# Four small moves in a fused attention and feed-forward kernel: first weight loads, idle products, the keys' cast, and where the first tile is stored

## The chip, the cores and the metric

One core of a Trainium2 chip runs the kernel. The metric is the device time of one execution in microseconds. The profile is of one execution; the times are medians of several. With one core there is no other core's clock to compare with, so a run counts as "fast" when it is within 1.5% of the fastest of its kernel; all comparisons below use fast runs.

## The reference, cut to what matters

```python
# q, k, v: (8, 8, 576, 64) float32: batch, heads, positions, head size
scores = (q @ k.transpose) / 8                      # only |i - j| <= 32 is kept
attn   = softmax(scores) @ v                        # to x: (4608, 512)
h      = x @ w_in                                   # 512 -> 2048
g      = gelu_tanh(h)
out    = g @ w_out                                  # 2048 -> 512, float32
```

The kernel works on nine tiles of 512 rows. While TensorE runs the feed-forward of tile t, the attention of batch t + 1 is woven in. Tiles 1 to 8 use Strassen's scheme (in Winograd's form) for w_out: sums of gT and of w_out are formed on VectorE ("sums", "combine"), and seven products replace eight. M1 is the first of these products.

Of the kernel before, what the change touches and what calls it, by code (L numbers as in the profile page):

```python
# [9 lines left out]
FP32 = mybir.dt.float32  # L10
FP16 = mybir.dt.float16
# [25 lines left out]
def cut(b):  # L37
    return 120 if b else 128
# [33 lines left out]
def kernel(  # L72
# [9 lines left out]
    nc = tc.nc  # L82
    B, H, S, D = q.shape
    DM, DF = moe_w_in.shape
    NTOK = B * S
    NPAIR = H // 2
# [15 lines left out]
    rawp = ctx.enter_context(tc.tile_pool(name="rawp", bufs=2))  # L102
    hp = ctx.enter_context(tc.tile_pool(name="hp", bufs=1))
# [16 lines left out]
    KTs = [const.tile([128, NPAIR, 512], FP16, name=f"KT{i}") for i in range(2)]  # L120
# [7 lines left out]
    raws = {}  # L128
# [76 lines left out]
    def stage_w():  # L205
        return stage.tile([128, 4, 512], FP32, name="wst", tag="stage")

    def load_w_in(i, w, c0=0, c1=4):
        nc.sync.dma_start(w[:, c0:c1, :], w_in_v[:, c0:c1, 512 * i:512 * i + 512])  # L209
        return w  # L210
# [18 lines left out]
    wi = []  # L229
    for i in range(4):  # L230
        wi.append(stage_w())
        for c0, c1 in ((0, 2), (2, 4)) if i else ((0, 1), (1, 2), (2, 4)):
            load_w_in(i, wi[i], c0, c1)

    idle = KTs[1][:, 0, 0:512]
    nc.vector.memset(idle, 0.0)
# [1 line left out]
    def spin(n, width=512, ps=None):  # L238
        ps = psO.tile([128, 512], FP32, name="spin", tag="O") if ps is None else ps
        for _ in range(n):  # L240
            nc.tensor.matmul(ps[:, 0:width], idle[:, 0:128], idle[:, 0:width], start=True, stop=True)
# [38 lines left out]
    def cast_open(b):  # L280
        halfs[b] = [hp.tile([128, NPAIR, 4, 2, 64], FP16, name="q16"),
                    hp.tile([128, NPAIR, 4, 2, 64], FP16, name="k16")]
        QTs[b] = ap_.tile([128, NPAIR, 4, 144], FP16, name="QT")
# [10 lines left out]
    def cast_v(b, c, copy=nc.gpsimd.tensor_copy):  # L294
        copy(Vs[b % 2][:, c, :, :], raws[b][3][:, c, :, :])
# [40 lines left out]
    def cast_and_turn(b):  # L336
        cast_open(b)
        q16, k16 = halfs[b]
        qr, kr, qt, kt = raws[b]
        qt16 = hp.tile([16, NPAIR, 4, 2, 64], FP16, name="qt16", tag="qt16")  # L340
        kt16 = hp.tile([64, NPAIR, 2, 64], FP16, name="kt16", tag="t16")
        def queries(src, dst, p0, p1):
            for pr in range(NPAIR):
                nc.vector.tensor_copy(
                    dst[:, pr, :, :, :].rearrange("p j h d -> p h j d"),
                    src[:, 2 * pr:2 * pr + 2, :].rearrange("p h (j d) -> p h j d", j=4))
            nc.sync.dma_start_transpose(QTs[b].rearrange("d r j p -> d (r j) p")[:, :, p0:p1],
                                        dst.rearrange("p r j h d -> p (r j h d)"))

        def rest(i):  # L350
            if i < NPAIR:
                nc.scalar.copy(qt16[:, i, :, :, :].rearrange("p j h d -> p h j d"),
                               qt[:, 2 * i:2 * i + 2, :].rearrange("p h (j d) -> p h j d", j=4))
            if i == 3:
                nc.sync.dma_start_transpose(QTs[b].rearrange("d r j p -> d (r j) p")[:, :, 128:144],
                                            qt16.rearrange("p r j h d -> p (r j h d)"))
            if i == 4:
                nc.scalar.copy(kt16.rearrange("p r h d -> p (r h d)"), kt.rearrange("p h d -> p (h d)"))
                nc.sync.dma_start_transpose(
                    KLs[b % 2], kt16.rearrange("p r h d -> p (r h d)"))  # L360
                raws[b].append(tailp.tile([64, H, 64], FP32, name="vt", tag="vt"))
                nc.sync.dma_start(raws[b][4], v[b, :, 512:S, :].rearrange("h p d -> p h d"))

        queries(qr, q16, 0, 128)
        if b == 2:
            combine(2, nc.vector)
        for pr in range(NPAIR):
            nc.vector.tensor_copy(k16[:, pr, :, :, :], kr[:, :, 2 * pr:2 * pr + 2, :])
            if pr % 2:
                nc.sync.dma_start_transpose(  # L370
                    KTs[b % 2][:, pr - 1:pr + 1, :].rearrange("d r (c p) -> d (r c) p", c=4),
                    k16[:, pr - 1:pr + 1, :, :, :].rearrange("p r c h d -> p (r c h d)"))
        if b == 2:
            vr = rawp.tile([128, 4, H, 64], FP32, name="qr")
            for c in range(4):
                nc.sync.dma_start(vr[:, c, :, :],
                                  v[b, :, 128 * c:128 * c + 128, :].rearrange("h p d -> p h d"))
        if b == 2:
            combine(3, nc.vector)
            combine(4, nc.vector)  # L380
            raws[b] = [None, None, None, vr]
            return rest
        queries(qt, qt16, 128, 144)
        nc.vector.tensor_copy(kt16.rearrange("p r h d -> p (r h d)"), kt.rearrange("p h d -> p (h d)"))
        nc.sync.dma_start_transpose(
            KLs[b % 2], kt16.rearrange("p r h d -> p (r h d)"))
# [54 lines left out]
    def times(b, g, o, pe, which=range(8)):  # L441
        m, prs, steps, slots, q0, n = work_of(b, g)
        for r, pr in enumerate(prs):
            cols = slice(4 * n * r, 4 * n * r + 4 * n)
            for slot, p0, p1 in slots:
                if slot not in which:
                    continue
                for h in range(2):
                    nc.tensor.matmul(  # L449
                        o[64 * h:64 * h + 64, cols].rearrange("d (j p) -> d j p", j=4)[:, :, p0 - q0:p1 - q0],  # L450
                        Vs[b % 2][:, slot, 2 * pr + h, :],
                        pe[:, h, cols].rearrange("k (j p) -> k j p", j=4)[:, :, p0 - q0:p1 - q0],
                        start=True, stop=True)
# [98 lines left out]
    def combine(i, eng):  # L552
        dst, x, y = wino["todo"][i]
        eng.tensor_tensor(dst, x, y, op=ALU.subtract)  # L554
# [14 lines left out]
    def store(t, t4, yo, cols=slice(0, 512), *engs):  # L569

        m = i = 0
        while m < 128:
            b, c = divmod(t * 512 + t4 * 128 + m, S)
            q0, n = (0, cut(b)) if c < 4 * cut(b) else (cut(b), 144 - cut(b))
            j, p = divmod(c - 4 * q0, n)
            e = min(n - p, 128 - m)
            nj = 1 if p else max(1, min(4 - j, (128 - m) // n))
            eng = engs[i % len(engs)] if engs else nc.gpsimd
            if nj > 1:
                e = nj * n  # L580
                eng.dma_start(out_v[b, j:j + nj, q0:q0 + n, cols], yo[m:m + e, cols])
            else:
                eng.dma_start(out_v[b, j, q0 + p:q0 + p + e, cols], yo[m:m + e, cols])  # L583
            m += e
            i += 1

    later = []
# [134 lines left out]
    s0 = psS.tile([128, 2, 512], FP32, name="ps_o", tag="S0")  # L722
# [3 lines left out]
    sums_of(3)  # L726
    os[3] = pieces("S1", "ps_o")
    times(0, 3, os[3], groups[(0, 3)], (0, 1, 4))
    spin(2, 512, s0[:, 1, :])
    for g in range(4):  # L730
        times(0, g, os[g], groups[(0, g)], (2, 5))
    spin(3, 512, s0[:, 1, :])
    cast_v(0, 3, nc.vector.tensor_copy)
    nc.vector.tensor_copy(Vs[0][odd, 7, :, :], Vs[0][odd, 3, :, :])
    nc.scalar.copy(Vs[0][even, 6, :, :], raws[0][3][even, 3, :, :])
# [59 lines left out]
    for t in range(NT):  # L795
        b = t + 1
        att = b < B
        if t:
            for fc in range(begun):
                ffn_in(t, fc, 3, 4, then=False)  # L800
            for fc in range(begun):
                gelu(t, fc)
            if att and b > 1:
                rest = cast_and_turn(b)
            for fc in range(begun, NF):
                ffn_in(t, fc)
                if t == 1 and fc in (3, 4, 5, 6):
                    cast_v(2, fc - 3)
                if t == 1 and 9 <= fc < 14:
                    rest(fc - 9)  # L810
                if t == 1 and fc == 8:
                    trans_tails(1, psO.tile([128, 8, 128], FP16, name="pt", tag="O"))
                if t > 1 and fc == 8 and att:
                    pair_v(b, nc.vector.tensor_copy)
# [10 lines left out]
        for i in range(113 if t else 65):  # L825
# [3 lines left out]
            for act in plan.get(i, "").split():  # L829
# [49 lines left out]
                elif kind == "v":  # L879
                    bb, gg = group(g)  # L880
                    o, d = weigh(bb, gg, at)
# [8 lines left out]
                cast_vt(2)  # L890
            if t == 1 and i in PAIR_1:
                pair_v(2, nc.vector.tensor_copy, PAIR_1[i])
            if t == 0 and i in (61, 62):
                store(0, *later.pop(0), slice(0, 512), nc.scalar)
            if t == 0 and i < 64:
                ffn_out_0(*ORDER_0[i])
            elif t and i < 112:
                ffn_out(t, i)
        if t == 0:
            for t4, yo in later:  # L900
                store(0, t4, yo)
            wino_rest(B12)
            load_table(gelu_set)
        else:
            ffn_last(t)
# [31 lines left out]
```

## The kernel before: the parts that the change touches

In the traces the engines follow the program's order, each for itself, and wait for one another's results: in the changed kernel GpSimd stands idle for 16.47 us ahead of a cast, with two finished results to store behind it for most of that time. A pool hands out buffers by tag; with one buffer per tag, a new tile is written only when what used the old one is done (in the changed kernel ScalarE waits 9.92 us for such a buffer). TensorE writes its products into banks (the tiles `mm` and `ph` of the lines); a new column starts only when its bank has been read out (there column 13 waits 9.12 us for gelu 10).

Results of tile 0, and where they lie (`hp` has one buffer per tag):

```python
def ffn_out_0(t4, fc):
    ...
    if fc == NF - 1:
        if "yo" not in pys:
            pys["yo"] = hp.tile([128, 2, 512], FP32, name="yo2", tag="qt16")
        yo = pys["yo"][:, t4, :] if t4 < 2 else yp.tile([128, 512], FP32, name="yo", tag="yo")
        (nc.scalar.copy if t4 > 1 else nc.vector.tensor_copy)(yo, pys[t4])
        later.append((t4, yo))                      # order: 0, 3, 1, 2
```

So results 0 and 1 lie in the buffer with the tag "qt16". Batch 2's query tails (positions 512 to 575 of the 576) take the same buffer next; SP is the queue that issues loads and transposes:

```python
def cast_and_turn(b):
    ...
    qt16 = hp.tile([16, NPAIR, 4, 2, 64], FP16, name="qt16", tag="qt16")
    ...
    def rest(i):
        if i < NPAIR:
            nc.scalar.copy(qt16[:, i, ...], qt[:, 2 * i:2 * i + 2, ...])
    ...
    queries(qr, q16, 0, 128)                        # VectorE casts, SP transposes
    combine(2)
    for pr in range(NPAIR):                         # keys
        nc.vector.tensor_copy(k16[:, pr, ...], kr[:, :, 2 * pr:2 * pr + 2, :])
        ...                                         # SP transposes, two pairs at a time
    ...                                             # SP loads batch 2's values (vr)
    combine(3); combine(4)
```

Tile 1, columns of w_in (16 of them; a gelu on ScalarE after each):

```python
for fc in range(begun, NF):
    ffn_in(t, fc)
    if t == 1 and fc in (3, 4, 5, 6):
        cast_v(2, fc - 3)                           # GpSimd, needs vr
    if t == 1 and 9 <= fc < 14:
        rest(fc - 9)                                # ScalarE
```

Stores of tile 0, at its end: ScalarE two, GpSimd two.

```python
if t == 0 and i in (61, 62):
    store(0, *later.pop(0), slice(0, 512), nc.scalar)
...
if t == 0:
    for t4, yo in later:
        store(0, t4, yo)                            # GpSimd
```

`spin(n)` issues n products of zeros, whose result nobody reads; it is meant to keep TensorE's clock up (with 40 of them in the stall, fill_again's granted clock was 1.00 from 70 to 84 us).

The softmax here doesn't subtract the row's maximum and nothing guards it: scores larger than these inputs give would overflow.

## Time and profile before

| | before |
|---|---|
| median of 3 runs | 302.96 us (302.71 to 306.03) |
| span of the profiled execution | 302.4 us |
| VectorE, ScalarE, GpSimd busy | 64%, 64%, 30% |
| first product with w_in / tile 1 / tile 2 begin | 20.71 / 58.29 / 92.69 us |

The last row is read from TensorE's order in time. These marks cut the kernel into stretches, so that a difference can be put in one of them. In the lines of this document, a group stands with its start, its duration, its engine and line, what it writes and reads, and in square brackets how long the engine idled before it and what ended that.

### The profile page before, as it was taken

The numbers are of one execution on the slowest core, as the hardware profiler recorded it, in microseconds if no ns is written. First come the engines' busy times: TensorE is split into PE (matmuls) and PEld (weight loads), VectorE is DVE, ScalarE is ACT, GpSimd is POOL, SyncE is SP. The second block draws the span as 40 slices with busy tenths as digits, with TensorE's granted clock in tenths as the row PEclk, the third lists the DMA queues.
The fourth block names the chain that finished last, engine by engine and source line by source line (L and its number), as shares of the span: only waits on it lengthen the run. The fifth ranks groups of instructions, "written<-read, shape, count | busy, mean of one in ns | idle before, by whom it ended". The sixth has DMA issues, their size and how long they took to land.

```text
span 302.4 us, 7120 instructions
## 1 busy us (share of the span) xinstructions
PE 290.0 (96%) x2896; PEld 179.8 (59%) x2896; DVE 194.6 (64%) x436; ACT 193.7 (64%) x307; POOL 91.3 (30%) x140
## 2 busy tenths in 40 slices
PE   8789899999799999999999999999999999999994
PEld 3444444445575478547854786478647864784583
DVE  4653648849969766876687668766876635543452
ACT  5855759389486695678566866686668666705600
POOL 3435527210546050606061506050620050015000
PEclk9979999999999999999999999999999999999998
DMA  7999999999799999698969996989594031004013
GB/s 220 231 304 379 319 332 243 270 244 209 179 212 178 187 220 170 124 175 197 175 134 156 241 170 144 154 211 173 83 197 54 3 86 55 2 0 140 2 37 102
DMA packets 116566, 50.73 MB, mean 168 GB/s; under 512 B 97927, under 2 KB 109959, under 8 KB 116534
## 3 DMA queue, kind: packets, MB, share of 16 engines
q1 hardware_dynamic: 87348, 37.88, 60.3%
q0 software_dynamic: 27776, 10.83, 25.3%
q10 hardware_dynamic: 1410, 1.58, 1.6%
q8 instruction: 22, 0.36, 0.5%
q14 instruction: 10, 0.08, 0.1%
HBM read 36.70 MB, written 9.44 MB: 153 GB/s over the span
## 4 chain that ended last, share of the span: by engine, by line
PE 71%; DMA 13%; SPq 7%; DVE 5%; POOL 1%; issue 1%; ACT 0%
PE mm L619 31%; PE mm L521 18%; PE ph L521 14%; DMA wst<-in_moe_w_out_dram 6%; DMA wst<-in_moe_w_in_dram 4%; SPq L175 3%; PE ps_s L416 3%; DVE s L564 2%; PE ps_d L439 2%; DMA qt<-in_q_dram 2%; SPq L209 2%; SPq L151 2%; PE ps_o L449 2%; DMA tr<-in_k_dram 2%; DVE t L554 1%
## 5 line engine op out<-in xcount | busy, mean ns | idle before, releaser
L521 PEld LDWEIGHTS <-w_in 128*128 128x128 f16 x576 | 56.2, 98 | 67.1 <-issue 1.4
L521 PE MATMUL mm<-xT,w_in 128*128 128x512 f16 x304 | 74.8, 379 | 0.4 <-DVE yo L599 0.4
L529 ACT ACTIVATE gT<-mm 128x512 f16<-128x512 f32 x76 | 45.1, 597 | 39.2 <-PE mm L521 38.5
L521 PE MATMUL ph<-xT,w_in 128*128 128x512 f16 x272 | 68.2, 379 | 0.1
L583 POOL DMA_DIRECT2D out_dram<-y x55 | 33.1, 610 | 89.2 <-DVE y L648 79.4
L619 PEld LDWEIGHTS <-s 128*128 128x128 f16 x512 | 49.3, 98 | 7.2 <-DVE s L564 1.2
L564 DVE TENSOR_TENSOR s<-gT 128x512 f16<-128x512 f16 x64 | 27.6, 432 | 34.7 <-ACT gT L529 34.7
L529 ACT ACTIVATE gT<-ph 128x512 f16<-128x512 f32 x68 | 37.9, 600 | 14.8 <-PE ph L521 14.8
L619 PE MATMUL mm<-t,s 128*128 128x256 f16 x376 | 45.2, 273 | 0.9 <-DVE s L564 0.9
L619 PEld LDWEIGHTS <-gT 128*128 128x128 f16 x384 | 35.8, 98 | 6.7
L428 ACT ACTIVATE pe<-ps_s 128x960 f16<-128x960 f32 (+1 forms) x32 | 30.4, 975 | 12.6 <-PE ps_s L416 12.5
L619 PE MATMUL mm<-w_out,gT 128*128 128x256 f16 x256 | 33.2, 273 | 0.8 <-DVE y L630 0.8
L97 ACT ACT_TABLE_LOAD x17 | 21.8, 1283 | 2.2 <-issue 1.9
L475 ACT ACTIVATE lt<-lt 128x480 f32<-128x480 f32 (+3 forms) x36 | 21.1, 585 | 1.1
L474 ACT ACTIVATE lt<-ps_d 128x480 f32<-128x480 f32 (+2 forms) x28 | 15.5, 555 | 9.0 <-PE ps_d L439 5.1
L434 DVE TENSOR_TENSOR pe<-pe,band 128x960 f16<-128x960 f16 x28 | 18.4, 680 | 1.0 <-ACT pe L428 1.0
L449 PEld LDWEIGHTS <-V 128*64 128x64 f16 x520 | 14.2, 115 | 7.5 <-DVE V L200 2.9
L183 POOL DMA_DIRECT2D V<-in_v_dram x20 | 17.9, 911 | 1.1 <-issue 0.4
L619 PE MATMUL mm<-t,gT 128*128 128x256 f16 x128 | 16.5, 273 | 0.0
L416 PEld LDWEIGHTS <-KT 64*64 64x64 f16 x576 | 10.1, 106 | 7.3 <-issue 5.7
L619 PE MATMUL mm<-w_out,s 128*128 128x256 f16 x120 | 14.4, 273 | 0.0
L564 DVE TENSOR_TENSOR s<-s,gT 128x512 f16<-128x512 f16 x32 | 13.6, 426 | 1.1
(109 smaller groups left out, 327.2 us busy)
## 6 DMA issues: line engine op xcount, KB each, us to landing
kr<-in_k_dram SPq DMA_DIRECT2D x31, 256.0 KB, 9.7
qr<-in_q_dram SPq DMA_DIRECT2D x6, 1024.0 KB
wst<-in_moe_w_in_dram SPq DMA_DIRECT2D x7, 512.0 KB, 9.3
wst<-in_moe_w_out_dram SPq DMA_DIRECT2D x3, 1024.0 KB, 11.1
V<-in_v_dram POOLq DMA_DIRECT2D x20, 128.0 KB, 8.5
vr<-in_v_dram SPq DMA_DIRECT2D x8, 256.0 KB, 5.4
qr<-in_q_dram SPq DMA_DIRECT2D x7, 256.0 KB
out_dram<-y POOLq DMA_DIRECT2D x6, 192.0 KB, 5.9
```

The costliest lines, as they stand in the source:

```text
L97: nc.scalar.add_instruction(mybir.InstLoadActFuncSet(name=nc.get_next_instruction_name(), act_func_set_id=which, ins=[], outs=[]))
L183: nc.gpsimd.dma_start(V[:, c, :, :], v[b, :, 128 * c:128 * c + 128, :].rearrange("h p d -> p h d"))
L416: nc.tensor.matmul(ps[64 * half:64 * half + 64, h, 4 * n * r:4 * n * r + 4 * n].rearrange("k (j p) -> k j p", j=4)[:, :, p0 - q0:p1 - q0], ...
L428: nc.scalar.activation(pe, ps[:, :, 0:w], AF.Exp, scale=SCALE)
L434: nc.vector.tensor_tensor(pe, pe, m.rearrange("k (o j) p -> k o j p", o=1).broadcast_to(list(pe.shape)), op=ALU.mult)
L449: nc.tensor.matmul(o[64 * h:64 * h + 64, cols].rearrange("d (j p) -> d j p", j=4)[:, :, p0 - q0:p1 - q0], Vs[b % 2][:, slot, 2 * pr + h, : ...
L475: nc.scalar.activation(lt[:, 0:n], lt[:, 0:n], AF.Exp, scale=-1.0)
L521: nc.tensor.matmul(ph, w_in16[:, dc, fc * 128:fc * 128 + 128], xT[:, dc, t * 512 % RING:t * 512 % RING + 512], start=(dc == 0), stop=(dc = ...
L529: nc.scalar.activation(gTs[t][:, fc, :], phs[fc], AF.Gelu_apprx_tanh)
L564: nc.vector.tensor_tensor(dst, x, y, op=op)
L583: eng.dma_start(out_v[b, j, q0 + p:q0 + p + e, cols], yo[m:m + e, cols])
L619: nc.tensor.matmul(pys["apart"][:, 0:256] if apart else py[:, blk, :], lhsT, wino[w][:, f, :], start=(new and i % (8 if one else 16) == 0) ...
```

## The change

The intent: two waits of TensorE shortened (last values, batch 2's sums), and tile 0's stores taken out of the time in which batch 2's keys are loaded. The diff, cut to its core:

```diff
-        for c0, c1 in ((0, 2), (2, 4)) if i else ((0, 1), (1, 2), (2, 4)):
-            load_w_in(i, wi[i], c0, c1)
+        for c0 in (0, 2):
+            load_w_in(i, wi[i], c0, c0 + 2)
 ...
-    spin(2, 512, s0[:, 1, :])
+    spin(3, 512, s0[:, 1, :])
     for g in range(4):
         times(0, g, os[g], groups[(0, g)], (2, 5))
-    spin(3, 512, s0[:, 1, :])
     cast_v(0, 3, nc.vector.tensor_copy)
 ...
         queries(qr, q16, 0, 128)
         if b == 2:
             combine(2, nc.vector)
+            combine(3, nc.vector)
+            return keys, rest              # keys(): casts, transposes, load of vr
 ...
                 ffn_in(t, fc)
-                if t == 1 and fc in (3, 4, 5, 6):
-                    cast_v(2, fc - 3)
+                if t == 1 and fc == 3:
+                    parts[0]()             # keys, behind sums 0
+                    combine(4, nc.vector)
+                if t == 1 and fc in (5, 6):
+                    store(0, *later.pop(0), slice(0, 512), nc.scalar)
+                if t == 1 and 6 <= fc < 10:
+                    cast_v(2, fc - 6)
+                if t == 1 and fc == 7:
+                    while later:
+                        store(0, *later.pop(0))
                 if t == 1 and 9 <= fc < 14:
-                    rest(fc - 9)
+                    parts[1](fc - 9)
 ...
-            if t == 0 and i in (61, 62):
-                store(0, *later.pop(0), slice(0, 512), nc.scalar)
 ...
-            for t4, yo in later:
-                store(0, t4, yo)
```

The tile qt16 is now taken from the pool at its first use (column 9), behind the stores in program order.

More of the change, by code (lines that the diff above doesn't have):

```diff
@@ L339, in cast_and_turn, with tails_of @@
         qr, kr, qt, kt = raws[b]
-        qt16 = hp.tile([16, NPAIR, 4, 2, 64], FP16, name="qt16", tag="qt16")
-        kt16 = hp.tile([64, NPAIR, 2, 64], FP16, name="kt16", tag="t16")
+        small = {}
+        def tails_of(which):
+            if which not in small:
+                small[which] = hp.tile([16, NPAIR, 4, 2, 64], FP16, name="qt16", tag="qt16") if which == "q" else \
+                    hp.tile([64, NPAIR, 2, 64], FP16, name="kt16", tag="t16")
+            return small[which]
         def queries(src, dst, p0, p1):
@@ L350, in rest @@
         def rest(i):
+            qt16, kt16 = tails_of("q"), tails_of("k") if i == 4 else None
             if i < NPAIR:
@@ L362, in rest, with keys @@
                 nc.sync.dma_start(raws[b][4], v[b, :, 512:S, :].rearrange("h p d -> p h d"))
+        def keys():
+            for pr in range(NPAIR):
+                nc.vector.tensor_copy(k16[:, pr, :, :, :], kr[:, :, 2 * pr:2 * pr + 2, :])
+                if pr % 2:
+                    nc.sync.dma_start_transpose(
+                        KTs[b % 2][:, pr - 1:pr + 1, :].rearrange("d r (c p) -> d (r c) p", c=4),
+                        k16[:, pr - 1:pr + 1, :, :, :].rearrange("p r c h d -> p (r c h d)"))
+            if b == 2:
+                vr = rawp.tile([128, 4, H, 64], FP32, name="qr")
+                for c in range(4):
+                    nc.sync.dma_start(vr[:, c, :, :],
+                                      v[b, :, 128 * c:128 * c + 128, :].rearrange("h p d -> p h d"))
+                raws[b] = [None, None, None, vr]
         queries(qr, q16, 0, 128)
@@ L366, in cast_and_turn @@
             combine(2, nc.vector)
-        for pr in range(NPAIR):
-            nc.vector.tensor_copy(k16[:, pr, :, :, :], kr[:, :, 2 * pr:2 * pr + 2, :])
-            if pr % 2:
-                nc.sync.dma_start_transpose(
-                    KTs[b % 2][:, pr - 1:pr + 1, :].rearrange("d r (c p) -> d (r c) p", c=4),
-                    k16[:, pr - 1:pr + 1, :, :, :].rearrange("p r c h d -> p (r c h d)"))
-        if b == 2:
-            vr = rawp.tile([128, 4, H, 64], FP32, name="qr")
-            for c in range(4):
-                nc.sync.dma_start(vr[:, c, :, :],
-                                  v[b, :, 128 * c:128 * c + 128, :].rearrange("h p d -> p h d"))
-        if b == 2:
             combine(3, nc.vector)
-            combine(4, nc.vector)
-            raws[b] = [None, None, None, vr]
-            return rest
+            return keys, rest
+        keys()
+        qt16, kt16 = tails_of("q"), tails_of("k")
         queries(qt, qt16, 128, 144)
@@ L803 @@
             if att and b > 1:
-                rest = cast_and_turn(b)
+                parts = cast_and_turn(b)
             for fc in range(begun, NF):
                 ffn_in(t, fc)
-                if t == 1 and fc in (3, 4, 5, 6):
-                    cast_v(2, fc - 3)
+                if t == 1 and fc == 3:
[8 more added lines that the diff above has]
+                        store(0, *later.pop(0))
                 if t == 1 and 9 <= fc < 14:
-                    rest(fc - 9)
+                    parts[1](fc - 9)
                 if t == 1 and fc == 8:
```

## The prediction

> **What bounds the kernel now.** I read the page first, then the waits of TensorE, then the order in time of each engine around the two places that the change touches (12 to 37 us, 58 to 82 us). The page and TensorE's waits:
>
> ```profile
> span 302.4 us, 7120 instructions
> PE 290.0 (96%) x2896; PEld 179.8 (59%) x2896; DVE 194.6 (64%) x436; ACT 193.7 (64%) x307; POOL 91.3 (30%) x140
> ...
> PE mm L449 <- DVE V L200: 2.1, 2, 1.2
> PE spin L241 <- DVE KT L236: 1.3, 1, 1.3
> PE mm L593 <- DVE w_out L218: 1.1, 2, 0.8
> PE mm L619 <- DVE s L564: 0.9, 1, 0.9
> PE mm L619 <- DVE y L630: 0.8, 1, 0.8
> ```
>
> TensorE is busy for 96% of the span. From 92.9 us to the end the chain that ended last is nearly all matmuls, and no part of the change lies there. So all that can be won is a few waits before 90 us: at most the 12.4 us that are not busy, of which these lines name 6.2. What can be lost has no such limit. Ahead of 58 us the loads set the pace. VectorE, then TensorE:
>
> ```profile
> 17.38 0.29 DVE L734 COPY V<-V 64x512 f16<-64x512 f16 x1
> ...
> 35.91 0.43 DVE L218 CAST w_out<-wst 128x512 f16<-128x512 f32 x1 [2.27 <-DMA wst<-in_moe_w_out_dram]
> ...
> 17.63 1.46 PE L241 MATMUL ps_o<-KT 128*128 128x512 f16 x3
> 19.02 0.50 PE L449 MATMUL mm<-pe,V 128*64 128x64 f16 x12
> ...
> 36.40 0.61 PE L593 MATMUL mm<-w_out,gT 128*128 128x512 f16 x2 [0.82 <-DVE w_out L218]
> ```
>
> The last values' copy ends at 17.67, but three products of zeros stand in front of the products that use it, which begin at 19.02. At 36.40 TensorE again waits for the first w_out, which is landing: what it arrives early at that point, it waits longer.
>
> In tile 1, VectorE, TensorE, GpSimd, ScalarE and the SP queue in turn:
>
> ```profile
> 66.82 1.43 DVE L368 CAST k<-kr 128x512 f16<-128x512 f32 x4 [4.37 <-issue]
> ...
> 70.44 0.42 DVE L564 TENSOR_TENSOR s<-gT 128x512 f16<-128x512 f16 x1
> ...
> 76.71 1.27 PE L619 MATMUL mm<-t,s 128*128 128x256 f16 x10 [0.94 <-DVE s L564]
> 78.80 0.27 PE L619 MATMUL mm<-w_out,gT 128*128 128x256 f16 x1 [0.83 <-DVE y L630]
> ...
> 60.28 1.38 POOL L583 DMA_DIRECT2D out_dram<-yo  x2 [3.18 <-DVE yo L599]
> 75.26 0.66 POOL L295 CAST V<-qr 128x512 f16<-128x512 f32 x1 [13.60 <-DMA qr<-in_v_dram]
> ...
> 67.84 0.60 ACT L352 CAST qt<-qt 16x512 f16<-16x512 f32 x1
> ...
> 62.42 5.28 SPq L347 DMA_TRANSPOSE QT<-q  x1
> 67.80 2.63 SPq L370 DMA_TRANSPOSE KT<-k  x2
> 70.48 4.45 SPq L376 DMA_DIRECT2D qr<-in_v_dram  x4
> ```
>
> VectorE stands still for 4.37 us until batch 2's keys have landed, although the first sums could run from about 63.1, when their fourth gelu ends. Then it is busy without a break to 78.7, and TensorE waits 0.94 us for a sum and 0.83 us for the copy of M1 behind it. GpSimd does nothing for 13.6 us, until the first chunk of batch 2's values lands at 75.26. ScalarE starts on qt16 at 67.84.
>
> [...] GpSimd issues the two stores itself (1.38 us). [...] The granted clock is 0.50 from 17.0 to 20.0 us here, after stalls of 1.2 and 0.9 us close together, and 1.00 again at 20.5. [...] From 58 to 67 us the three queues take 79.3%, 17.3% and 15.9%, so the four stores of tile 0 do share the engines with the keys. [...] The four stores took 5.6 to 6.1 us to land; those after 90 us 3.6 to 7.3, median 4.4.
>
> **The change part by part.**
>
> First weights in two loads: one issue less on SP (0.43 to 0.5 us), the same bytes. The first chunk now lands with the second, 18.73 instead of 18.06; its cast (0.61) ends at 19.34. The loads' queue is full (100.5% of 16 engines' time over the first 60 us), so an issue less moves nothing later. 0.
>
> No zeros ahead of the last values: two spins go. The final products start near 17.7 instead of 19.02 and w_in's matmuls near 19.4 instead of 20.7, some of that lost if the clock is still at half. At 36.40 TensorE waits for w_out, which lands with the bytes ahead of it, at 35.91 as before: its wait grows from 0.82 to about 2 us. 0 at the end, at best 0.3.
>
> Sums ahead of the keys: sums 0 (four of 0.34 us, 1.4) run at about 63.6 to 65.0, in VectorE's 4.37 us gap. Combine 3 (1.2) also moves into it. The queue behind the keys falls from 11.9 us (66.82 to 78.75) by 2.6, so that the last sum is done soon after the last gelu and M1 is copied in time. Both waits go: 0.94 + 0.83 = 1.8 us, and the two small ones after (0.16 and 0.19, on V and xT) partly: 2.1 us gained.
>
> Tile 0's stores inside tile 1: half of its results lie in the slot that qt16 uses next (one buffer, tag "qt16"): results 0 and 1. The order in which they finish is 0, 3, 1, 2. ScalarE now stores 0 and 3 after gelus 5 and 6; GpSimd stores 1 and 2 at column 7. But on GpSimd two casts of batch 2's values stand ahead of them (columns 6 and 7), and these wait for loads that SP issues after the keys' transposes. So: ScalarE at column 9 must write qt16, which waits for result 1's store, which waits for GpSimd's second value cast. When?
> - Queries' transpose: 62.42 + 5.28 before. With fewer stores beside it, an estimate of 62.2 + 4.4 (others of it took 2.8 to 5.3, median 3.9) = 66.6.
> - Two keys' transposes, 2.63: 69.2. The keys land earlier, by the stores' part in the engines' time, and are cast by 66.5.
> - Values: before, 70.48 to the second chunk's cast at 76.25 were 5.8 us. So 75.1, cast 0.6: 75.7.
> - Store of result 1: issue to landing about 4: 79.7.
>
> ScalarE reaches qt16 at 79.7 instead of 67.84, and gelus 10 to 15 stand behind it. TensorE can still run columns 10, 11 and 12 (three banks), stops near 70.6, and goes on when gelu 10 has freed a bank: 79.7 + 0.6 + 0.6 = 80.9. [...] It ends at 85.2, where it was at 72.33: +12.8 us. The exponentials follow ScalarE's last gelu by the same distance as before, and TensorE asks for them no earlier. Nothing later in the chain waits on less, so the delay stays to the end.
>
> Sum: 12.8 − 2.1 = +10.7, so 302.96 + 10.7 = 313.7; I say 313.5 us.
>
> **The rivals.**
>
> One: the wait on qt16 doesn't bind, because the values land much earlier or the stores do. Then the change gives 1.8 to 2.1 us, at best 3 with a bit from the spins: 300 to 301.2, "same". For it: the step is made to look like tidying, and whoever writes such a change measures it. Against it: the SP queue works in order and the queries' transpose alone holds it to 66 or 67.7. Even with nothing in the way the second value chunk is not there before 73.5, ScalarE is due at 67.8.
>
> Two: only the part of qt16 under result 1 waits. Its first two pieces lie under result 0, stored by ScalarE at about 64.3, landed near 69 to 70. Then ScalarE stops at the third piece, two gelus later. TensorE gets two columns further, the stall is about 2 us shorter: 310.5 to 312. Against it: the buffer is released as a whole; before qt16 ScalarE has two extra semaphore waits at 67.5 us in the present trace.
>
> Three: the delay is larger. Stores of ScalarE now fall beside the transposes and the loads of the values; if these slow down, or the store takes 6 to 7 us, 316 to 318.
>
> Four: a loss at the start through fewer spins, with the clock at half for longer. The w_out wait at 36.40 swallows up to 2 us of it: no more than 0.5 us.
>
> **Range and chances.** The stall's length is good to about 3 us either way, mostly from the value's landing (73.5 to 77.5) and the store (3 to 6). With rival two inside, 307.0 to 319.0 should hold 8 in 10. Slower by over 2% means over 309.0: 0.83. Within 2%: 0.14, mostly rival one. Faster by over 2% would need 6.1 us, more than all the waits that the change touches: 0.03.
>
> **What would show it.** Right: a wait of ScalarE of 9 to 13 us ahead of its first copy to qt16; TensorE idle from about 70.6 with the clock at 0.50 after it; GpSimd's stores after its second value cast, at 75 to 77. Sums 0 ahead of the keys' cast, and no wait for a sum or M1 after. A longer wait for w_out at 36.4. From 100 us on everything as before, shifted by 9 to 12 us. Wrong: the first qt16 copy near 68, or GpSimd's stores before its value casts, or a start of tile 1's matmuls that moved by over 1 us.

## The result, and the profile after

The changed kernel takes 313.84 us (median of 4 runs, 313.03 to 314.56) against 303.59 of the kernel before in the same rounds. The ratio is 1.0324, 95% interval 1.0256 to 1.0392: slower. Ratios here are the mean time of one kernel's fast runs over that of the other's fast runs of the same rounds, so they are not quite the ratio of the medians.

The page of the changed kernel, and who waited for whom on TensorE and then on ScalarE (total us, times, longest):

```profile
span 312.8 us, 7121 instructions
...
PE 291.1 (93%) x2894; PEld 179.9 (58%) x2894; DVE 194.3 (62%) x436; ACT 194.2 (62%) x307; POOL 90.8 (29%) x140
```

```profile
PE mm L530 <- ACT gT L538: 9.1, 1, 9.1
PE mm L458 <- DVE V L200: 1.8, 2, 1.0
PE mm L602 <- DVE w_out L218: 1.5, 2, 1.2
```

```profile
ACT qt L359 <- DMA out_dram<-yo: 9.9, 1, 9.9
```

TensorE is as busy as before in microseconds (291 against 290). What is new is one wait of 9.1 us for a gelu, and one of 9.9 us of ScalarE for a store of tile 0, ahead of its first copy into qt16. The waits for a sum and for M1 are gone. The chain that ended last, in order of time, shows how the two hang together:

```profile
69.26 4.24 DMA qr<-in_v_dram
...
73.62 0.55 POOL V L295
74.17 2.99 DMA out_dram<-yo
...
77.23 0.62 ACT qt L359
77.85 0.50 ACT gT L538
...
78.39 3.57 PE mm L530 x8
```

It reads: batch 2's values land (qr is the buffer's name), GpSimd casts the second chunk, and only then issues the store of result 1. The store lands, qt16 becomes free, ScalarE copies, runs gelu 10, and TensorE gets a bank back. TensorE, GpSimd and SP in the same stretch, each as its own order in time:

```profile
68.24 1.03 PE L530 MATMUL ph<-xT,w_in 128*128 128x512 f16 x4
78.39 3.57 PE L530 MATMUL mm<-xT,w_in 128*128 128x512 f16 x8 [9.12 <-ACT gT L538]
81.75 1.91 PE L530 MATMUL ph<-xT,w_in 128*128 128x512 f16 x4
83.46 1.65 PE L628 MATMUL mm<-w_out,gT 128*128 128x256 f16 x10
...
72.14 0.61 POOL L295 CAST V<-qr 128x512 f16<-128x512 f32 x1 [16.47 <-DMA qr<-in_v_dram]
...
74.17 1.29 POOL L592 DMA_DIRECT2D out_dram<-yo  x2
...
61.59 3.67 SPq L353 DMA_TRANSPOSE QT<-q  x1
65.35 3.10 SPq L375 DMA_TRANSPOSE KT<-k  x2
68.50 3.78 SPq L381 DMA_DIRECT2D qr<-in_v_dram  x4
```

GpSimd stood idle for 16.47 us, for most of them with two finished results to store, because a cast that had nothing to cast yet stood in front. Twelve matmuls of columns 13 to 15 then take 5.1 us (78.39 to 83.46), twice as long as the last twelve of tile 1 in the kernel before (69.74 to 72.33, 2.6 us). The granted clock by stretches is the third number from the end of each line, ahead of the DMA share:

```profile
73.00:74.00 1.00, 0.00 (x0) 0.00 (x0) 0.00 (x0) 0.00 (x0) 0.38 (x1) 1.00 1.31 219
74.00:75.00 1.00, 0.00 (x0) 0.00 (x0) 0.00 (x0) 0.00 (x0) 1.00 (x3) 0.50 0.86 139
...
83.50:84.00 0.50, 0.50 (x4) 0.38 (x3) 0.00 (x0) 0.29 (x1) 0.00 (x0) 0.50 0.03 0
84.00:84.50 0.50, 0.50 (x5) 0.39 (x4) 0.17 (x1) 0.48 (x2) 0.00 (x0) 0.75 0.42 78
```

So the clock was full until 74 us, though TensorE had stood still since 69.3, and at half from there to about 84.25.

Where the 10.4 us between the two spans lie, by the marks of the section on the time before:

| stretch | before | after | difference |
|---|---|---|---|
| start to tile 1 | 58.29 | 57.66 | −0.63 |
| tile 1 to its first product with w_out | 14.04 | 25.80 | +11.76 |
| from there to tile 2 | 20.36 | 18.87 | −1.49 |
| tile 2 to the end | 209.71 | 210.47 | +0.76 |

The loss is all in one stretch. Whether the two gains belong to the change is a question for the experiments.

### The profile page after: what moved, and what is told of

Same layout as the page of the kernel before. It is cut to its first block, busy times and chain, and to the rows that moved or that the text cites.

```text
span 312.8 us, 7121 instructions
## 1 busy us (share of the span) xinstructions
PE 291.1 (93%) x2894; PEld 179.9 (58%) x2894; DVE 194.3 (62%) x436; ACT 194.2 (62%) x307; POOL 90.8 (29%) x140
## 4 chain that ended last, share of the span: by engine, by line
PE 66%; DMA 20%; SPq 7%; DVE 3%; POOL 1%; issue 1%; ACT 1%; DVEq 0%; ACTq 0%; POOLq 0%
PE mm L628 30%; PE mm L530 15%; PE ph L530 12%; DMA wst<-in_moe_w_out_dram 5%; DMA KT<-k 5%; DMA wst<-in_moe_w_in_dram 4%; PE ps_s L425 3%; SPq L175 2%; PE ps_d L448 2%; SPq L209 2%; SPq L151 2%; DMA tr<-in_k_dram 2%; PE ps_o L458 2%; DMA kr<-in_k_dram 2%; DMA qr<-in_v_dram 1%; DMA out_dram<-yo 1%
## 5 line engine op out<-in xcount | busy, mean ns | idle before, releaser
L530 PE MATMUL mm<-xT,w_in 128*128 128x512 f16 x304 | 76.4, 386 | 9.2 <-ACT gT L538 9.1
L530 PE MATMUL ph<-xT,w_in 128*128 128x512 f16 x272 | 69.2, 383 | 0.2
L573 DVE TENSOR_TENSOR s<-gT 128x512 f16<-128x512 f16 x64 | 26.9, 420 | 48.6 <-ACT gT L538 48.6
L425 PE MATMUL ps_s<-QT,KT 64*64 64x128 f16 (+3 forms) x576 | 13.8, 216 | 0.8 <-DMA KT<-k 0.6
```

The source lines that it names most:

```text
L425: nc.tensor.matmul(ps[64 * half:64 * half + 64, h, 4 * n * r:4 * n * r + 4 * n].rearrange("k (j p) -> k j p", j=4)[:, :, p0 - q0:p1 - q0], ...
L530: nc.tensor.matmul(ph, w_in16[:, dc, fc * 128:fc * 128 + 128], xT[:, dc, t * 512 % RING:t * 512 % RING + 512], start=(dc == 0), stop=(dc = ...
L573: nc.vector.tensor_tensor(dst, x, y, op=op)
```

## The experiments

My theory: the loss is the wait for the buffer under qt16, which GpSimd's late store of result 1 holds ("slot theory"). Rivals: the moved stores slow tile 1's loads by their traffic; the keys' new place delays the values; the half clock after the stall is a large part. And the gains: do the waits for a sum and for M1 really go because of the change? All outputs are right.

**own_slot**: the changed kernel, results 0 and 1 elsewhere.

```diff
-            pys["yo"] = hp.tile([128, 2, 512], FP32, name="yo2", tag="qt16")
+            pys["yo"] = rawp.tile([128, 2, 512], FP32, name="yo2", tag="kr")
```

> The changed kernel, but results 0 and 1 of tile 0 lie in a buffer that qt16 doesn't take (a free slot of the raw keys). Stores, casts and their order are as in the changed kernel. Slot theory (ScalarE waits for the slot under qt16, which GpSimd's late store holds): the 9.9 us wait ahead of the first qt16 copy and TensorE's 9.1 us idle both go, 300.3 to 302, at or a little under the kernel before. Traffic theory (stores inside tile 1 slow the loads and transposes there, wherever they read from): stays at 311 to 314.

Measured: 302.44 us against 303.96, ratio 0.9954 (0.9929 to 0.9978), 0.4 us above my range. One of 20 runs counts as slow; with it, the means are still 0.4% apart. ScalarE's and GpSimd's lines:

```profile
67.27 0.60 ACT L359 CAST qt<-qt 16x512 f16<-16x512 f32 x1
...
74.60 1.29 POOL L592 DMA_DIRECT2D out_dram<-yo  x2
```

GpSimd's stores are as late as in the changed kernel (74.60 against 74.17), but nobody waits for them: qt16 is written at 67.27 with no wait noted. The whole loss is gone: 1.0324 over 0.9954 is 1.037, some 11 us between two kernels that differ only in where two results lie. The traffic theory falls, since the same bytes go at the same time.

**swap**: the changed kernel; ScalarE stores results 0 and 1, GpSimd 2 and 3.

```diff
+                if t == 1 and fc == 5:
+                    later.sort(key=lambda r: r[0])
                 if t == 1 and fc in (5, 6):
```

> The changed kernel, but ScalarE stores results 0 and 1 (the ones in the slot that qt16 takes) after gelus 5 and 6, and GpSimd stores 2 and 3, still behind its second value cast at about 74 us. Slot theory: qt16 then waits only for ScalarE's own stores, issued at 63.1 and 64.0 and landing 3 to 5 us later, so a wait of 0.5 to 2.5 us in place of 9.9, and 301 to 304 in all, although GpSimd's stores are as late as before. Theory that GpSimd's late stores cost time by themselves (traffic, or value casts pushed back by them): 311 to 314.

Measured: 303.5 against 303.96, ratio 0.9985 (0.9961 to 1.0010); one of 13 runs, of 309.64 us, counts as slow.

```profile
68.97 0.62 ACT L359 CAST qt<-qt 16x512 f16<-16x512 f32 x1 [1.81 <-DMA out_dram<-yo]
...
74.28 1.29 POOL L592 DMA_DIRECT2D out_dram<-yo  x2
```

The buffers are those of the changed kernel; only which engine stores which result differs. The wait shrinks from 9.92 to 1.81 us, as expected, and the loss is gone again. So it is neither the sharing of the buffer alone nor GpSimd's late stores alone, but both on the same result.

**stores_only**: the kernel before with the stores and the value casts moved, and qt16 taken at its first use, as the change has it (not shown in the cut).

```diff
-                if t == 1 and fc in (3, 4, 5, 6):
-                    cast_v(2, fc - 3)
+                if t == 1 and fc in (5, 6):
+                    store(0, *later.pop(0), slice(0, 512), nc.scalar)
+                if t == 1 and 6 <= fc < 10:
+                    cast_v(2, fc - 6)
+                if t == 1 and fc == 7:
+                    while later:
+                        store(0, *later.pop(0))
```

> The kernel before with the stores of tile 0 and the value casts moved to where the change has them, and nothing else: keys ahead of the sums, three loads of the first weights, spins as they were. Slot theory: the whole loss and no gain, slower than the kernel before by 11 to 14 us (314 to 317), because the change's other parts won some 2.5 us. Theory that it takes the keys' new place to delay the values: 302 to 305.

Measured: 313.64 against 303.96, ratio 1.0320 (1.0297 to 1.0343). Its waits of TensorE and of ScalarE:

```profile
PE mm L529 <- ACT gT L537: 9.1, 1, 9.1
...
ACT qt L359 <- DMA out_dram<-yo: 9.9, 1, 9.9
```

The cause is sufficient by itself, and the keys' place has no part in it. But I had expected more than the whole change, because the other parts should have won 2.5 us. It is the same as the whole change: those gains do not show.

**stores_back, keys_only, spins_only, loads_only**: the other parts. stores_back is the changed kernel with the stores at their old place; the three others are the kernel before with one part of the change each. stores_back and keys_only also keep the change's later value casts (columns 6 to 9) and its late taking of qt16.

```diff
 # stores_back: the changed kernel, and
-                if t == 1 and fc in (5, 6): store(...)      # ScalarE, and GpSimd's at fc == 7
+            if t == 0 and i in (61, 62): store(...)         # and GpSimd's at the end of tile 0
 # keys_only: the kernel before, and
+                if t == 1 and fc == 3: parts[0](); combine(4, nc.vector)
+                if t == 1 and 6 <= fc < 10: cast_v(2, fc - 6)
 # spins_only: the kernel before, and spin(2) -> spin(3) ahead of slots (2, 5), no spin ahead of the last
 # loads_only: the kernel before, and two loads of the first weights in place of three
```

> The changed kernel with tile 0's stores where they were before (issued at the end of tile 0, ahead of the value casts), all else of the change kept. My sum without the stall: 0.6 from an earlier start of tile 1 plus 1.8 to 2.1 from the two waits for a sum and for M1, so faster than the kernel before by 1.8 to 2.7 us, near 300.5. No wait on a store ahead of qt16 of over 0.5 us. Rival (the stores in tile 0 were in the keys' way, so that moving them is what freed VectorE): the keys land near 66.8 again, and the gain is under 1 us.

> The kernel before with batch 2's keys cast behind the first sums and nothing else. Sums theory: TensorE's waits for a sum (0.94) and for M1 (0.83) go, faster by 1.5 to 2.1 us. Rival (the waits only move to the values, which land no earlier): faster by under 0.7 us, with a new wait on the value casts or on the scores.

> The kernel before with three products of zeros ahead of the middle values and none ahead of the last. Prediction's claim: w_in's matmuls start 1.3 to 1.8 us earlier, the wait for w_out at 36.4 swallows it, 0 to 0.3 us at the end. Rival: what the changed kernel's trace shows, a start of tile 1 that is 0.6 us earlier, comes from here: faster by 0.5 to 0.8 us.

> The kernel before with the first weights in two loads in place of three and nothing else. Prediction's claim: the first chunk is cast 0.5 to 0.7 us later, nothing waits for that, and the time is the same within 0.2 us. Rival: one issue less lets all later loads land 0.4 us earlier, and as the loads set the pace to 58 us, 0.3 to 0.6 us faster.

| kernel | median | before | ratio | 95% interval |
|---|---|---|---|---|
| stores_back | 303.09 | 303.71 | 0.9990 | 0.9969 to 1.0012 |
| keys_only | 303.50 | 303.71 | 0.9993 | 0.9972 to 1.0015 |
| spins_only | 303.36 | 303.71 | 0.9980 | 0.9962 to 0.9998 |
| loads_only | 304.27 | 303.71 | 1.0011 | 0.9987 to 1.0034 |

All are within 0.2%. spins_only can be told from nothing, barely (0.6 us by its ratio, 0.35 by the medians), and it is one of four; whether my 0 to 0.3 or its rival, 0.5 to 0.8, is nearer is not settled. loads_only bears out "the same", but not how: the first chunk was cast at 18.1 us as before, since the two chunks now land by 18.1, not by 18.7. stores_back wins 0.3 us, where I had 1.8 to 2.7; its rival has the size right but not the reason, since the keys were cast at 65.13, not near 66.8. keys_only wins nothing that these rounds can show, where I had 1.5 to 2.1 us. Its rival fits: the wait on V for the first products with the values is 0.7 us in its trace, where the kernel before had 0.2. And spins_only and loads_only, which have the old order in tile 1, show neither the wait for a sum nor that for M1. That led to the next run.

**before_again**: the kernel before, unchanged, for a second profile (one run, so its state is unknown).

> The kernel before once more, unchanged, for another profile. Its first profile has the keys of batch 2 cast at 66.8 us and TensorE waiting 0.94 us for a sum and 0.83 us for M1; two kernels with the same order of work in tile 1 (three products ahead of the middle values; first weights in two loads) show the keys at 65.0 and 65.3 and neither wait. If the waits belong to that one execution and not to the kernel: keys at 65 to 65.5 here too and under 0.3 us of those two waits together. If they belong to the kernel: 1.5 us or more of them again.

Measured: 304.4 us, span 302.6, the keys 0.15 us later than the first expectation and neither wait. TensorE's waits, then VectorE's cast of the keys:

```profile
PE mm L593 <- DVE w_out L218: 1.6, 2, 1.3
PE ps_s L416 <- DMA KT<-k: 1.3, 1, 1.3
...
PE ps_od L449 <- DVE V L193: 0.9, 1, 0.9
...
65.65 1.43 DVE L368 CAST k<-kr 128x512 f16<-128x512 f32 x4 [2.99 <-DMA kr<-in_k_dram]
```

The waits for a sum and for M1 (1.8 us) do not stand among the waits of this execution. The keys landed 1.2 us earlier (65.65 against 66.82), so VectorE had its sums done in time. In their place TensorE waited 0.9 us for the values and 1.3 us for a later batch's transposed keys, which the first profile hadn't. The span is the same to 0.2 us. So those 1.8 us do not belong to every execution, and where they were missing here, other waits for loads took as much. Against this second profile, the changed kernel's stretches differ by −0.85, +11.76, −0.18 and −0.53: so the gain of 1.49 between w_out and tile 2 is not shown to be a property of the change. Over all profiles, that stretch takes 19.0 to 20.4 us in the four with the old order of keys and sums and no stall, and 18.3 to 19.1 in the five with the new order and no stall or a short one. Up to a microsecond may be won there, but the times of keys_only and stores_back do not show it.

**fill** and **fill_again**, with **after_again** beside the latter: the changed kernel, and TensorE's idle time filled with 40 products of no use (spin's operand holds batch 1's keys by then, no longer zeros), so that its clock stays up; and the changed kernel itself once more.

```diff
+                if t == 1 and fc == 13:
+                    spin(40)
                 ffn_in(t, fc)
```

> The changed kernel with 40 products of no use (0.216 us each at full clock, 8.6 us) ahead of column 13, in TensorE's idle time. ScalarE's wait stays at 9 to 10 us. If half of the clock after the stall is a real part of the loss: columns 13 to 15 take 0.86 us each, ScalarE's last gelu comes 1 us earlier, and 311.3 to 312.5 come out in place of 313.8. If ScalarE alone sets the pace after the stall: 313.5 to 314.5.

> The changed kernel once more, beside the next one on one chip: 1.030 to 1.034 of the kernel before, ScalarE's wait on the store of result 1 9 to 11 us.

> The changed kernel with 40 products in TensorE's idle time, once more, because its first profile had the values 1.2 us later than the changed kernel's and four runs settle nothing. From the first qt16 copy to the first product of w_out it took 4.1 us there against 6.2 in the changed kernel. If that is worth time: 1.5 to 2.3 us under the changed kernel of the same rounds. If the fill itself delays the values, or the time is won back by nobody: within 0.7 us of it.

Measured: fill 313.95 us, 1.0306 (1.0263 to 1.0348; one of four runs, of 318.39, counts as slow); after_again 313.85 us, 1.0327 (1.0280 to 1.0373); fill_again 313.66 us, 1.0334 (1.0291 to 1.0377). fill_again's lines of ScalarE and TensorE:

```profile
79.93 0.62 ACT L359 CAST qt<-qt 16x512 f16<-16x512 f32 x1 [11.03 <-DMA out_dram<-yo]
...
81.08 2.02 PE L530 MATMUL mm<-xT,w_in 128*128 128x512 f16 x8 [1.59 <-ACT gT L538]
```

From the first qt16 copy to the first product with w_out it is 4.1 us in both fills, and 6.2 and 5.7 in the changed kernel's two profiles. The granted clock is 1.00 from 70 to 84 us in fill_again, and 1.00 on the mean of the whole profiled run in fill. So the half clock costs 1.6 to 2.1 us there. But the time doesn't fall, and of my two expectations for fill the slower one came, for another reason (fill_again too is within 0.7 us of the changed kernel): in both fills the values come later. From the keys' cast to the first value cast it takes 9.3 and 9.6 us, against 7.8 in both profiles of the changed kernel. From tile 1 to the first product with w_out it is 24.9 and 24.8 us in the fills, 25.8 and 25.0 in the changed kernel. Whether the 40 products delay the values is not shown: the fills are the slowest of the 14 profiles, but the other ten take 7.1 to 8.7, 7.1 in late_stores, whose TensorE works all through, and 8.4 in stores_only, whose TensorE stands still. So I claim the 1.6 to 2.1 us only for that stretch, not for the kernel's time.

**late_stores**: own_slot, and all four stores on GpSimd behind its last value cast.

```diff
-                if t == 1 and fc in (5, 6):
-                    store(0, *later.pop(0), slice(0, 512), nc.scalar)
-                if t == 1 and fc == 7:
+                if t == 1 and fc == 10:
                     while later:
                         store(0, *later.pop(0))
```

> Results 0 and 1 in a buffer of their own as in own_slot, and all four stores of tile 0 on GpSimd behind its last value cast (about 77 us). ScalarE issues none, the values are cast with no store between. If the stores between the value casts cost anything in own_slot (0.9 us of waiting for V there): faster than the kernel before by 1.5 to 2.5 us. If TensorE then only waits longer for the next keys' transpose (1.0 us in own_slot): as own_slot, 0.5% faster.

Measured: 301.89 us against 303.85, ratio 0.9938 (0.9913 to 0.9963). By its fast runs it is 1.9 us faster than the kernel before, inside the first expectation. But five of its 22 runs (304.79 to 308.07) count as slow, because its fastest, 300.11, lies so low, while the kernel before with runs up to 306.33 loses none. Over all runs the means are 302.72 and 303.67: about 1.0 us apart, with an estimated 95% interval of −0.1 to 1.9 from their scatter. So a typical execution is faster, but a gain in the mean is not shown, and own_slot, in other rounds with an interval that overlaps, can't be told from it. The four stores land 8.0 to 8.6 us after their issue, and nothing waits for them. The wait for V is 0.3 us (0.9 in own_slot), that for the transposed keys 0.7 (1.0).

## Why the prediction was right

313.5 was predicted, 313.84 measured, inside 307 to 319, and "slower" is what came. By its steps:

- **What bounds the kernel.** Right that loads pace the start, at least up to the first w_out: TensorE's first product with w_out begins between 35.8 and 36.8 us in 13 of the 14 profiles (37.7 in fill_again), while the first product with w_in begins anywhere from 18.76 to 20.72. Wrong in one reading: I took the 0.94 and 0.83 us of one profile for properties of the kernel.
- **Two loads, and no zeros ahead of the last values: 0, at best 0.3.** Nearly right. The second chunk landed with the first, not the first with the second: both were cast from 18.1 us, not from 18.7. w_in's products began at 18.96 (19.4 predicted) and the wait for w_out grew from 0.82 to 1.18, less than the 2 us predicted, for the most part since w_out came 0.4 earlier and a wait of 0.6 for a cast of the next batch's keys lay between. The part about spins is worth 0.2% by its ratio (0.1% by the medians), at the edge of what can be told.
- **Sums ahead of the keys: −2.1 us.** This step failed. In the trace the mechanism shows (sums 0 run ahead of the keys' cast, and the two waits are gone), but keys_only wins 0.07% with an interval of ±0.2%, and before_again has no such waits without the change.
- **The stores.** The mechanism was right in every link: order on GpSimd, the buffer, ScalarE's queue, TensorE's banks. Own_slot and swap break one link each, and the loss goes; stores_only has it alone. The sizes: queries' transpose done 65.3 (66.6), keys' transposes 68.4 (69.2), second value cast done 74.2 (75.7), store landed 3.0 us later (4.0), first qt16 copy 77.23 (79.7), TensorE on again 78.39 (80.9), first product with w_out 83.46 (85.2), the predicted ones in brackets. So the stall ended 1.7 us earlier, and this and the missing gain of 2.1 us cancelled to within 0.4: that the total is closer to the truth than its terms is luck. Two slips in the working, without effect: TensorE stopped at 69.3, not 70.6 (three columns of 0.86 back from 72.33 are 69.7), and the 5.6 to 6.1 us to land are those of GpSimd's two stores, not of all four, as the trace has no landing for ScalarE's.
- **Half clock after the stall.** The 4.3 us for the three columns (80.9 to 85.2) were my estimate; no trace at hand showed how long the clock stays at half after a long stall. It lasted from 78.39 to about 84.25 in one profile, 5.9 us, and from 78.51 to about 82.55 in the other, 4.0 us, with no idle time of TensorE noted in between, and the three columns took 5.1 and 4.6 us. The clock had fallen 4.7 and 2.6 us after TensorE's last product (69.3 to 74.0, and 69.7 to 72.3). In the kernel before it was at 0.50 from 17.0 to 20.0 us, after waits of only 1.2 and 0.9 us, and at 1.00 from 20.5. What sets these lengths is not shown.
- **Rivals.** One (the wait doesn't bind) is refuted by the 9.9 us. Two (only the pieces under result 1 wait) as well: ScalarE stopped at the first piece, under result 0, and went on when GpSimd's store had landed (74.17 + 2.99, qt16 at 77.23). Three and four did not come.

What stays open: whether the 40 products made the values come later, and what else moves the landing of the same loads by a microsecond or two from one profile to the next: from the keys' cast to the first value cast it took 7.1 to 9.6 us over the 14 profiles. Nor is it shown what sets the time of GpSimd's stores of 256 KB: they landed after 3.0 to 3.2 us in the changed kernel, 5.6 to 6.1 in the kernel before, and 8.0 to 8.6 in late_stores.

## What to carry to other kernels

Ahead of moving a store, look at which buffer it reads, who takes that buffer next, and what stands in front of the store in its engine's queue: a store behind a cast that waits for a load can hold a third engine (9.9 us of ScalarE here, and 9.1 of TensorE behind it). A store that goes late from a buffer that nobody needs holds up nothing: in own_slot GpSimd's are issued at 74.60, in late_stores the four land 8.0 to 8.6 us after their issue, and nothing waits. And do not take a wait of one microsecond in one profile for a property of the kernel before a second profile has it too: here it sat at another place the next time.
